# Attention with a gated MLP on one core: seven products one batch earlier, a weight load in halves, zeros multiplied in early waits, a new table of moments

## The chip, the core and the metric

The kernel runs on one core of a Trainium2 chip. The metric is the device time of one execution in microseconds, the median of several runs. The engines are TensorE (PE in the rows; PEld is its weight load), VectorE (DVE), ScalarE (ACT), GpSimd (POOL) and SyncE (SP), which issues most transfers.

## The reference

The reference is causal windowed attention, a gated layer and a spatially gated MLP, one behind the other, for 8 batches of 576 positions and 8 heads of 64:

```python
scores = scale * np.matmul(q, k.transpose(0, 1, 3, 2))   # heads 0-3: window of 32; 4-7: 32 keys, every 4th
attn = softmax(np.where(masks, scores, -1e9));  x = attn @ v          # (B, S, 512)
gate = sigmoid(causal_conv5(x, conv_w));  y = (gate * (x @ w_val)) @ w_out_1
h = relu(y @ w_in);  u, v = h[..., :512], h[..., 512:]
v_n = (v - mean(v)) / sqrt(var(v) + 1e-6)
v_s = einsum('ts,bsd->btd', w_spatial, v_n) + b_spatial[None, :, None]
out = (u * v_s) @ w_out_2
```

The weight matrices (w_val, w_out_1, w_in, w_out_2, conv_w) come as 64-bit floats, 1 MB for each half of a matrix of 512x512; q, k, v and w_spatial are 32-bit.

## The kernel before

A batch goes through two parts. Its attention (`a_...`) takes the 8 heads as 4 pairs: `a_scores` (72 small products into one PSUM buffer `s`), `a_max` (VectorE: scale, mask, row maximum), `a_exp` (ScalarE), `a_sum` (VectorE, then a multiplication on POOL), `a_trans` (in batch 0 products with the identity on TensorE and eight ScalarE copies; later VectorE and small transfers), `a_pv`, `a_split` (a value as a high part that TensorE takes in one pass and a low rest), `a_conv` (five VectorE steps, each on the result of the one before) and `a_tanh`. Then the MLP: `val` (8 tiles of 128x288; in batch 0 four float32 products each, later twelve of high and low parts), `v` and `norm` (5 row blocks), `u`, `sp`, and last `out`.

The last product, with w_out, is done in one of two ways. Up to batch `SEVEN - 1`, `out` does 8 tiles with 12 products each, and ScalarE copies each tile out and stores it. From batch `SEVEN` on the 2x2 block matrix is multiplied with seven block products instead of eight: `sp` subtracts two blocks more, `t` makes three combinations of blocks on VectorE with their high and low parts, `w` does 14 groups of six products, whose results VectorE adds up. `wsum` makes the sums of w_out's blocks that this needs, once.

Weights are loaded in two units each (`load_w`), converted from 64 bits by one ScalarE step (Abs) and four VectorE steps (`from64`, used by `w_f32`, each step on the result of the one before), and for batch 0 two of them are multiplied with each other (`fuse`: w_out_1 with w_in, so that the layer between them falls away; `wm` is w_out_1, in the trace `w_mid`, `wiv` and `wiu` the two halves of w_in, `wv` is w_val).

The order of everything is written out by hand. Each step is a generator; a part runs up to its next `yield`. `EARLY` gives a moment for each part of each step of the first batches, `EVERY` for all later ones (shifted by 74.5 a batch). The loop at the end takes the part with the lowest moment, emits its instructions, and puts the next part back with the higher of its own moment and the one just used. Every engine, and the sync queue with its transfers, then works in exactly the order of emission. Moments have no other meaning: they only sort.

The PSUM pool `ps_m` (tag `m`) has four buffers, which `val`, `v`, `u`, `sp`, `out`, `w`, `fuse` and batch 0's `a_trans` share; `s` and `o` have one buffer each. `qk` and `vv` have two buffers each; unit 0 of `wiu` is loaded into the place of unit 0 of `wv`. In the profile all instructions have line 641, that of the wrapper that records them, so the rows are told apart by their tiles.

Of the kernel before, what the change touches and what calls it, by code (L numbers as in the profile page):

```python
# [28 lines left out]
SEVEN = 2  # L29
# [34 lines left out]
def _swapped(b, x):  # L64
# [11 lines left out]
ORDER = [  # L76
    ("load_qk", 0, 0),
# [111 lines left out]
    ("w_f32", "wiv", 0,): (3.801, 6.907, 7.863, 8.102, 8.341,),
    ("a_sum", 0, 0,): (4.279, 5.951,),  # L190
    ("load_w", "wm", 1,): (4.518,),
    ("a_scores", 0, 1,): (4.757,),
    ("conv_w_f32",): (4.996, 6.668, 7.146, 7.624, 10.013,),
    ("a_max", 0, 1,): (5.235, 5.474,),
    ("a_exp", 0, 1,): (5.712,),
    ("a_pv", 0, 0,): (6.190, 12.403, 15.987,),
    ("load_qk", 0, 2,): (6.429,),
    ("a_trans", 0, 0,): (7.385, 8.819, 9.774, 10.252, 10.730,),
    ("w_f32", "wm", 1,): (8.580, 11.447, 12.642, 15.748, 16.226,),
    ("a_scores", 0, 2,): (9.058,),  # L200
    ("load_mask", 1,): (9.297,),
    ("a_pv", 0, 3,): (9.536, 36.775, 37.253,),
    ("fuse", "wiv", 0,): (10.491, 11.686, 19.571, 20.288, 23.872, 25.783,),
    ("load_w", "wiv", 1,): (10.969,),
    ("a_conv", 0, 0,): (11.208, 17.421, 20.049, 21.721, 22.199, 23.394,),
    ("a_sum", 0, 1,): (11.925, 12.881,),
    ("load_vv", 0, 0,): (12.164,),
    ("a_trans", 0, 1,): (13.120, 13.359, 16.465, 19.810, 20.766,),
    ("a_pv", 0, 1,): (13.598, 25.067, 27.695,),
    ("a_max", 0, 2,): (13.836, 14.075,),  # L210
    ("load_qk", 0, 3,): (14.314,),
    ("a_scores", 0, 3,): (14.553,),
# [12 lines left out]
    ("a_trans", 0, 2,): (22.677, 24.111, 25.306, 25.545, 26.978,),
    ("w_f32", "wv", 0,): (22.916, 23.155, 24.350, 26.739, 28.173,),
    ("a_scores", 1, 0,): (23.633,),
    ("a_exp", 0, 3,): (24.589,),
    ("load_vv", 1, 0,): (24.828,),
    ("fuse", "wiv", 1,): (26.022, 26.261, 27.217, 27.456, 28.412, 30.084,),  # L230
    ("a_sum", 0, 3,): (28.651, 30.562,),
    ("load_bias",): (28.890,),
    ("fuse", "wiv", 2,): (29.129, 31.757, 32.235, 33.907, 38.686, 45.616,),
    ("val", 0, 0, 0,): (29.607, 32.713, 33.191, 37.731, 41.793, 43.943, 45.855,),
    ("a_trans", 0, 3,): (31.040, 31.518, 34.624, 35.341, 35.580,),
    ("a_conv", 0, 1,): (31.279, 33.669, 38.925, 40.598, 47.766,),
    ("a_tanh", 0, 0,): (32.952,),
    ("a_conv", 0, 2,): (33.430, 35.819, 37.969, 40.120, 41.554,),
    ("load_mask", 2,): (34.146,),
    ("load_qk", 1, 2,): (34.385,),  # L240
    ("val", 0, 2, 0,): (34.863, 38.447, 42.270, 42.987, 46.571, 47.527, 56.129,),
    ("load_mask", 3,): (35.102,),
    ("load_w", "wiu", 0,): (36.058,),
    ("a_max", 1, 0,): (36.297, 39.642,),
    ("load_vv", 0, 3,): (36.536,),
    ("a_pv", 1, 1,): (37.014, 87.669, 95.076,),
    ("a_scores", 1, 1,): (37.492,),
    ("val", 0, 1, 0,): (38.208, 39.881, 41.315, 43.465, 49.200, 53.740, 56.607,),
    ("load_w", "wiu", 1,): (39.164,),
    ("a_pv", 1, 0,): (39.403, 73.333, 75.722,),  # L250
    ("w_f32", "wiu", 0,): (40.359, 42.509, 46.332, 48.483, 49.439,),
    ("a_conv", 0, 3,): (40.837, 44.421, 47.288, 50.155, 51.589,),
    ("load_qk", 2, 1,): (41.076,),
    ("val", 0, 3, 0,): (42.031, 44.899, 46.810, 49.678, 55.651, 57.085, 59.952,),
    ("load_sp", 4,): (42.748,),
    ("a_tanh", 0, 2,): (43.226,),
    ("val", 0, 1, 1,): (43.704, 47.049, 49.917, 51.111, 52.545, 57.802, 73.094, 84.563,),
    ("a_exp", 1, 0,): (44.182,),
    ("load_sp", 2,): (44.660,),
    ("split_pair", "wm", 0,): (45.138, 53.979, 61.147, 62.580,),  # L260
    ("val", 0, 3, 1,): (45.377, 48.005, 48.961, 50.872, 54.217, 60.191, 75.483, 89.581,),
    ("load_vv", 1, 2,): (46.093,),
    ("a_tanh", 0, 1,): (48.244,),
    ("split_sp", 4,): (48.722, 68.315, 69.988, 83.129, 83.846, 99.138,),
    ("a_sum", 1, 0,): (50.394, 53.023,),
    ("val", 0, 0, 1,): (50.633, 51.350, 51.828, 52.306, 55.173, 56.846, 68.554, 70.943,),
    ("split_pair", "wiu", 0,): (52.067, 53.262, 54.695, 60.669,),
    ("val", 0, 2, 1,): (52.784, 54.934, 57.324, 57.563, 59.713, 71.421, 72.138, 78.112,),
    ("a_tanh", 0, 3,): (53.501,),
    ("w_f32", "wiu", 1,): (54.456, 58.279, 59.474, 60.908, 61.864,),  # L270
    ("a_trans", 1, 0,): (55.412, 55.890, 56.368, 59.235, 64.253,),
    ("load_sp", 1,): (58.040,),
    ("split_pair", "wm", 1,): (58.518, 63.058, 63.297, 63.536,),
    ("fuse", "wiu", 1,): (58.757, 65.209, 67.359, 68.793, 69.749, 74.288,),
    ("fuse", "wiu", 2,): (58.996, 64.492, 69.271, 75.244, 78.350, 80.501,),
    ("v", 0, 1,): (60.430, 61.386, 64.970, 70.226,),
    ("a_max", 1, 1,): (61.625, 62.819,),
    ("split_pair", "wiu", 1,): (62.102, 62.341, 65.448, 67.598,),
    ("v", 0, 0,): (63.775, 64.731, 70.465, 71.660,),
    ("fuse", "wiu", 3,): (64.014, 66.164, 67.120, 74.050, 77.873, 80.262,),  # L280
    ("fuse", "wiu", 0,): (65.687, 66.642, 67.837, 69.032, 71.899, 78.589,),
    ("a_exp", 1, 1,): (65.926,),
    ("load_sp", 0,): (66.403,),
    ("a_sum", 1, 1,): (66.881, 69.510,),
    ("split_pair", "wv", 1,): (68.076, 76.439, 76.917, 91.970,),
    ("load_vv", 1, 1,): (70.704,),
    ("a_conv", 1, 0,): (71.182, 75.005, 79.545, 81.935, 84.324, 87.191,),
    ("split_sp", 2,): (72.377, 83.607,),
    ("a_scores", 1, 2,): (72.616,),
    ("a_trans", 1, 1,): (72.855, 73.572, 75.961, 76.678, 80.023,),  # L290
    ("split_sp", 0,): (73.811, 85.997,),
    ("load_qk", 1, 3,): (74.527,),
    ("norm", 0, 0,): (74.766, 76.200, 85.041,),
    ("norm", 0, 1,): (77.156, 77.395, 77.634,),
# [392 lines left out]
def attention_gated_mlp_kernel(  # L687
# [902 lines left out]
```

## Time and profile before

| | us |
|---|---|
| median of 3 runs | 649.7 |
| lowest, highest | 648.9, 651.69 |
| the profiled execution | 648.66 |
| its span, first to last instruction | 646.9 |

The profile is that of one execution. The time of that execution is its span and 1.8 us around it. Rows of TensorE need care: a product's duration includes its way through the array, so products that follow each other overlap, and the price of one is the duration of a block divided by its number.

### The profile page before, as it was taken

What the parts mean: (1) busy time and instruction counts of PE and PEld (TensorE: products, weight loads), DVE (VectorE), ACT (ScalarE), POOL (GpSimd) and SP (SyncE); (2) the same over time, 40 slices, a digit from 0 to 9 for tenths busy, and PEclk for the clock granted to TensorE, in tenths of its full rate; (3) what the DMA queues carried; (4) which work ended last, traced back from release to release, by engine and by line L of the source; (5) the groups of instructions that cost most, each with busy time, mean ns of one, the idle gap of its engine ahead of it and who ended that gap; (6) DMA issues with size and microseconds to landing.
All of it is one profiled execution on the core that took longest, in us unless ns stands there. A gap on an engine that the chain in (4) does not pass through costs nothing.

```text
span 646.9 us, 18122 instructions
## 1 busy us (share of the span) xinstructions
PE 626.2 (97%) x7176; PEld 578.5 (89%) x7176; DVE 489.7 (76%) x883; ACT 351.0 (54%) x994; POOL 349.6 (54%) x418
## 2 busy tenths in 40 slices
PE   2899999999999999999999999999999999999997
PEld 2557889998899989999899989999899989999997
DVE  4999878987788787786687967787687967774425
ACT  4967678624444435545476656555476656443422
POOL 1112898746635574575546456375547456455524
PEclk9999999999999999999999999999999999999999
DMA  8953235344331611144213431144214421110002
GB/s 323 412 197 118 56 108 198 113 130 99 80 81 36 184 19 20 41 143 125 76 42 125 118 105 47 19 150 118 75 41 126 119 72 42 19 49 28 2 1 74
DMA packets 85609, 63.61 MB, mean 98 GB/s; under 512 B 64531, under 2 KB 74643, under 8 KB 85013
## 3 DMA queue, kind: packets, MB, share of 16 engines
q1 hardware_dynamic: 76884, 53.60, 28.1%
q10 hardware_dynamic: 8640, 8.85, 3.9%
q8 instruction: 57, 0.93, 0.6%
q14 instruction: 28, 0.22, 0.1%
HBM read 44.92 MB, written 9.44 MB: 84 GB/s over the span
## 4 chain that ended last, share of the span: by engine, by line
PE 92%; DMA 2%; DVE 2%; POOL 1%; ACT 1%; issue 0%; ACTq 0%; SPq 0%; DVEq 0%
PE sp_ps L641 19%; PE u_ps L641 16%; PE v_ps L641 16%; PE val_ps L641 14%; PE w_ps L641 14%; PE o_ps L641 5%; PE s_ps L641 4%; PE out_ps L641 4%; DMA raw<-in_w_mid_t 1%; DMA out<-ob 1%; DVE wiv_f L641 1%; DVE wm_f L641 1%; POOL gl L641 1%; DVE w_sum L641 0%; PE t_ps L641 0%
## 5 line engine op out<-in xcount | busy, mean ns | idle before, releaser
L641 DVE SCALAR_TENSOR_TENSOR tt<-xt,cw,tt 128x576 f32<-128x576 f32 x116 | 104.9, 910 | 13.6 <-ACT tt L641 10.9
L641 PE MATMUL sp_ps<-wsp_h,vh 128*128 128x288 f32 x320 | 93.5, 297 | 0.0
L641 POOL TENSOR_TENSOR g2l<-ru,g2h 128x288 fp32r<-128x288 f32 x64 | 60.5, 961 | 56.5 <-ACT g2h L641 47.6
L641 PE MATMUL u_ps<-gl,w_h 128*128 128x288 f32 x256 | 75.6, 295 | 1.2 <-POOL gl L641 1.2
L641 POOL TENSOR_TENSOR gl<-tt,gh 128x288 fp32r<-128x288 f32 x64 | 56.3, 890 | 37.3 <-ACT gh L641 37.1
L641 PE MATMUL u_ps<-gh,w_h 128*128 128x288 f32 x256 | 76.0, 297 | 0.0
L641 PE MATMUL sp_ps<-wsp_l,vh 128*128 128x288 f32 x256 | 75.4, 295 | 0.0
L641 PE MATMUL sp_ps<-wsp_h,vl 128*128 128x288 f32 x256 | 75.4, 295 | 0.0
L641 PE MATMUL u_ps<-gh,w_l 128*128 128x288 f32 x256 | 75.4, 294 | 0.0
L641 ACT ACTIVATE e_t<-e_t,mx 128x64 f32<-128x64 f32 x207 | 68.9, 336 | 3.4 <-DVE mx L641 2.1
L641 POOL TENSOR_TENSOR e_t<-e_t,sm 128x576 f32<-128x576 f32 x31 | 39.2, 1266 | 56.4 <-DVE sm L641 36.0
L641 PE MATMUL val_ps<-xh,wval_h 128*128 128x288 f32 x224 | 66.7, 298 | 0.2 <-DVE tt L641 0.2
L641 PE MATMUL val_ps<-xh,wval_l 128*128 128x288 f32 x224 | 66.0, 295 | 0.0
L641 PE MATMUL val_ps<-xl,wval_h 128*128 128x288 f32 x224 | 66.0, 294 | 0.0
L641 PEld LDWEIGHTS sp_ps<-wsp_h,vh 128*128 128x128 f32 x320 | 60.0, 188 | 0.8
L641 PE MATMUL v_ps<-w_h,gh 128*128 128x512 f32 x160 | 58.8, 392 | 0.0
L641 PE MATMUL v_ps<-w_l,gh 128*128 128x512 f32 x160 | 58.5, 390 | 0.0
L641 POOL TENSOR_TENSOR rs<-rs,mhalf 128x1 f32<-128x1 f32 x40 | 26.6, 666 | 52.1 <-DVE rs L641 49.4
L641 POOL TENSOR_TENSOR xl<-xt,xh 128x576 fp32r<-128x576 f32 x28 | 42.4, 1516 | 20.8 <-ACT xh L641 20.8
L641 ACT CAST g2h<-ru 128x288 fp32r<-128x288 f32 x64 | 27.0, 432 | 48.5 <-DVE ru L641 34.9
L641 POOL TENSOR_TENSOR vl<-v_t,vh 128x512 fp32r<-128x512 f32 x32 | 43.3, 1362 | 12.9 <-ACT vh L641 12.3
L641 PEld LDWEIGHTS u_ps<-gl,w_h 128*128 128x128 f32 x256 | 48.0, 188 | 2.2 <-POOL gl L641 1.7
(163 smaller groups left out, 1839.0 us busy)
## 6 DMA issues: line engine op xcount, KB each, us to landing
qk_t<-in_qk SPq DMA_DIRECT2D x30, 592.0 KB, 4.3
vv_t<-in_vv SPq DMA_DIRECT2D x30, 384.0 KB, 4.7
out<-ob ACTq DMA_DIRECT2D x38, 144.0 KB, 2.0
raw<-in_w_in SPq DMA_DIRECT2D x4, 1024.0 KB, 8.3
pt<-et SPq DMA_DIRECT2D x240, 16.0 KB, 1.9
out<-ru ACTq DMA_DIRECT2D x22, 144.0 KB, 2.9
pt<-et SPq DMA_DIRECT2D x144, 20.0 KB, 1.8
raw<-in_w_mid_t SPq DMA_DIRECT2D x2, 1024.0 KB, 10.4
```

Of the source, the lines that this page charges most:

```text
L641: ins = self._tc.keep_in_program_order(fn(*args, **kwargs))
```

## The change

Five things are changed.

- `SEVEN` is 1 instead of 2: batch 1, too, does its last product with `t` and `w` in place of `out`, and `wsum` comes in batch 1.
- The load of unit 0 of `wm` is issued as two transfers of 512 KB, and its conversion is done in two halves, ten parts in place of five.
- A tile `zero` of 128x288 is set to zero by VectorE first of all; `warm` multiplies it with itself, 16 times in all, in nine steps, each into a buffer of `ps_m` that nobody reads.
- Every moment in `EARLY` is replaced; `EVERY` is as before. Many parts now have a moment below that of the part ahead of them (often below zero), which makes them follow at once.
- Some entries of `EARLY` go (`out` of batch 1), others come (`wsum`, `warm`).

```diff
-SEVEN = 2
+SEVEN = 1
 ORDER = [
+    ("warm", 0, 2),
...
+    ("warm", 7, 1),
+    ("warm", 8, 1),
     ("load_qk", 0, 0),
...
 EARLY = {
-    ("load_w", "wm", 0,): (0.217,),
-    ("load_ident",): (1.412,),
-    ("w_f32", "wm", 0,): (1.889, 2.367, 3.084, 3.562, 4.040,),
-    ("a_exp", 0, 1,): (5.712,),
-    ("w_f32", "wm", 1,): (8.580, 11.447, 12.642, 15.748, 16.226,),
-    ("a_conv", 0, 2,): (33.430, 35.819, 37.969, 40.120, 41.554,),
-    ("w_f32", "wiu", 0,): (40.359, 42.509, 46.332, 48.483, 49.439,),
...
+    ("warm", 0, 2,): (-133.081,),
+    ("load_w", "wm", 0,): (-73.526, -75.209,),
+    ("warm", 5, 2,): (-56.644,),
+    ("warm", 7, 1,): (-53.220,),
+    ("a_scores", 0, 0,): (-52.205,),
+    ("load_w", "wm", 1,): (-25.599,),
+    ("load_qk", 0, 2,): (-25.305,),
+    ("load_qk", 0, 3,): (-22.397,),
+    ("load_ident",): (-21.606,),
+    ("w_f32", "wm", 0,): (-21.389, -63.873, -71.475, -69.879, -56.098, -100.527, -22.399, -78.854, -44.988, -26.893,),
+    ("a_exp", 0, 0,): (-20.865,),
+    ("w_f32", "wm", 1,): (-2.766, -53.646, -82.714, -12.021, 12.392,),
+    ("a_exp", 0, 1,): (8.085,),
+    ("a_conv", 0, 2,): (39.452, -20.612, -11.415, -61.458, -14.711,),
+    ("w_f32", "wiu", 0,): (40.027, 41.020, 39.149, 47.579, 51.578,),
+    ("a_tanh", 0, 0,): (40.227,),
+    ("a_pv", 0, 3,): (-22.569, 45.022, -30.396,),
+    ("wsum", 1,): (141.159, 148.262, 116.586, 142.348, -3.076,),
+    ("wsum", 3,): (195.850, 138.468, 7.495, 144.068, 125.820,),
...
+            if (key, u) == ("wm", 0):
+                raw[key, u] = t
+                syn.dma_start(out=t[:, 0], in_=src[:, 0])
+                yield
+                syn.dma_start(out=t[:, 1], in_=src[:, 1])
+                return
...
+    def warm(i, n):
+        ps = ps_m.tile([128, 512], F32, tag="m", name="warm_ps")
+        for k in range(n):
+            matmul(ps[:, 0:HS], zero[:, 0:128], zero, True, True)
...
+        if (key, u) == ("wm", 0):
+            a, b = (from64(wide[key][:, m, 0:DM], raw[key, u][:, m]) for m in range(2))
+            for _ in a:
+                yield
+            yield
+            yield from b
+            return
...
+    zero = act.tile([128, S], F32, tag="ru0", name="zero")[:, 0:HS]
+    vec.memset(zero, 0.0)
```

## Rows read from the trace of the kernel before

**Rows 1.** The page, part 1: busy time, share of the span, instructions.

```profile
PE 626.2 (97%) x7176; PEld 578.5 (89%) x7176; DVE 489.7 (76%) x883; ACT 351.0 (54%) x994; POOL 349.6 (54%) x418
```

**Rows 2.** Busy time by stretch: stretch, its length, each engine, granted clock, DMA share.

```profile
0.00:8.00 8.00, 2.16 (x72) 1.92 (x72) 1.32 (x3) 1.28 (x1) 1.89 (x7) 1.00 0.71 229
8.00:16.00 8.00, 2.16 (x72) 1.95 (x72) 5.41 (x9) 5.36 (x21) 0.91 (x1) 1.00 1.02 417
16.00:31.00 15.00, 11.79 (x273) 8.17 (x274) 14.52 (x25) 14.40 (x57) 1.80 (x6) 1.00 1.02 418
31.00:72.00 41.00, 40.62 (x432) 28.59 (x432) 40.47 (x60) 27.88 (x83) 13.34 (x12) 1.00 0.43 143
...
128.00:250.00 122.00, 120.57 (x1367) 112.63 (x1366) 97.27 (x164) 49.72 (x102) 71.08 (x81) 1.00 0.33 88
250.00:600.00 350.00, 350.00 (x3978) 332.40 (x3977) 262.11 (x500) 196.04 (x585) 193.53 (x245) 1.00 0.28 78
600.00:647.00 47.00, 43.01 (x311) 41.92 (x309) 20.33 (x46) 14.87 (x33) 18.77 (x21) 1.00 0.08 26
```

**Rows 3.** TensorE in order of time: start, duration, instructions, idle before and its end.

```profile
4.50 2.16 PE L641 MATMUL s_ps<-qk_t 64*32 64x64 f32 x72 [4.50 <-DMA qk_t<-in_qk]
11.19 2.16 PE L641 MATMUL s_ps<-qk_t 64*32 64x64 f32 x72 [4.54 <-DMA qk_t<-in_qk]
...
19.20 2.16 PE L641 MATMUL s_ps<-qkv 64*32 64x64 f32 x72 [1.19 <-DVE wiv_f L641]
...
30.71 3.70 PE L641 MATMUL w_ps<-wiv_f,wm_f 128*128 128x512 f32 x8 [1.73 <-DVE wiv_f L641]
...
49.73 1.03 PE L641 MATMUL s_ps<-qk_t 64*32 64x64 f32 x72
```

**Rows 4.** The chain that ended last: start, duration, work.

```profile
51.13 13.85 PE val_ps L641 x56
...
66.38 5.45 PE v_ps L641 x24
...
202.93 8.19 PE out_ps L641 x60
...
211.58 3.21 DMA out<-ob
...
226.56 1.31 POOL w_sums L641
```

**Rows 5.** Waits of TensorE from 225 to 250 us: total, times, longest.

```profile
PE u_ps L641 <- POOL gl L641: 1.2, 2, 0.6
```

**Rows 6.** Transfers issued at 1.65, 3.6, 4.76 and 40 to 50 us: size, us to landing.

```profile
raw<-in_w_mid_t SPq DMA_DIRECT2D x1, 1024.0 KB, 7.8
raw<-in_w_in SPq DMA_DIRECT2D x1, 1024.0 KB, 10.1
raw<-in_w_mid_t SPq DMA_DIRECT2D x1, 1024.0 KB, 12.9
raw<-in_w_in SPq DMA_DIRECT2D x2, 1024.0 KB, 6.4
```

**Rows 7.** VectorE in order of time, as rows 3.

```profile
10.67 1.42 DVE L641 TENSOR_SCALAR wm_f<-wm_f 128x1024 f32<-128x1024 f32 x2 [2.42 <-ACT wm_f L641]
...
31.58 0.74 DVE L641 SCALAR_TENSOR_TENSOR e_t<-s_ps,mask_sb 128x576 f32<-128x576 f32 x1
32.24 0.81 DVE L641 SCALAR_TENSOR_TENSOR tt<-o_ps,cw,tt 128x576 f32<-128x576 f32 x1
32.97 0.74 DVE L641 TENSOR_REDUCE mx<-e_t 128x9 f32<-128x576 f32 x1
...
64.58 0.41 DVE L641 SCALAR_TENSOR_TENSOR tt<-tt,val_ps 128x288 f32<-128x288 f32 x1
...
88.55 1.66 DVE L641 SCALAR_TENSOR_TENSOR tt<-o_ps,cw,tt 128x576 f32<-128x576 f32 x2
```

**Rows 8.** VectorE by form: count, busy us, mean ns, idle before.

```profile
L641 DVE TENSOR_TENSOR ru<-ru 128x288 f32<-128x288 f32 x48 | 33.4, 716 | 2.1
...
L641 DVE TENSOR_TENSOR ru<-w_ps,ru 128x288 f32<-128x288 f32 x48 | 20.2, 451 | 4.9 <-PE w_ps L641 4.7
```

More of the change, by code (lines that the diff above doesn't have):

```diff
@@ L76 @@
 ORDER = [
+    ("warm", 0, 2),
+    ("warm", 1, 2),
+    ("warm", 2, 2),
+    ("warm", 3, 2),
+    ("warm", 4, 2),
+    ("warm", 5, 2),
+    ("warm", 6, 2),
+    ("warm", 7, 1),
+    ("warm", 8, 1),
     ("load_qk", 0, 0),
@@ L253 @@
[L253 to L270, printed above, removed]
@@ new lines @@
+    ("warm", 6, 2,): (8.995,),
+    ("load_w", "wv", 1,): (9.227,),
+    ("a_scores", 0, 3,): (9.920,),
+    ("a_sum", 0, 1,): (10.347, 13.354,),
+    ("a_max", 0, 2,): (11.066, -59.406,),
+    ("load_vv", 0, 1,): (12.331,),
+    ("w_f32", "wiv", 1,): (14.326, 3.954, -34.884, -44.589, -35.744,),
+    ("a_exp", 0, 2,): (14.337,),
+    ("a_pv", 0, 0,): (15.469, 5.567, -28.107,),
+    ("load_sp", 0,): (16.631,),
+    ("warm", 4, 2,): (17.412,),
+    ("a_sum", 0, 2,): (17.436, -46.083,),
+    ("load_qk", 1, 0,): (18.886,),
@@ new lines @@
+    ("fuse", "wiv", 1,): (29.101, 35.839, -11.970, -103.245, -62.727, -16.098,),
+    ("fuse", "wiv", 3,): (29.808, -26.519, 35.425, -19.764, -53.811, -45.761,),
+    ("load_vv", 0, 3,): (30.938,),
+    ("warm", 8, 1,): (31.235,),
+    ("load_w", "wiu", 0,): (31.277,),
+    ("a_trans", 0, 2,): (31.900, -107.608, -14.237, -17.687, -7.412,),
+    ("load_qk", 2, 0,): (32.905,),
+    ("load_mask", 2,): (33.692,),
+    ("a_pv", 1, 0,): (36.129, 73.298, -39.382,),
+    ("a_scores", 1, 0,): (37.699,),
@@ new lines @@
+    ("a_exp", 1, 0,): (51.102,),
+    ("a_sum", 1, 0,): (53.227, 5.437,),
+    ("val", 0, 3, 1,): (54.066, 61.463, 27.924, -72.217, -17.183, -114.819, 65.728, 5.826,),
+    ("val", 0, 1, 1,): (54.410, 58.507, 9.188, 25.180, -27.228, 64.645, 9.054, -104.737,),
+    ("val", 0, 0, 1,): (54.924, 55.792, 21.716, 27.762, -26.212, -11.445, -18.340, -0.934,),
+    ("load_w", "wiu", 1,): (55.652,),
+    ("a_tanh", 0, 1,): (57.241,),
+    ("split_pair", "wiu", 0,): (57.995, -8.850, -156.658, -10.448,),
+    ("load_vv", 1, 0,): (59.497,),
@@ new lines @@
+    ("a_tanh", 0, 3,): (60.412,),
+    ("a_scores", 1, 1,): (60.630,),
+    ("a_trans", 1, 0,): (60.939, -24.411, -74.118, -15.202, -6.561,),
+    ("load_sp", 2,): (61.283,),
+    ("val", 0, 1, 0,): (61.592, 45.798, 41.191, 56.575, -29.116, 47.475, -35.541,),
+    ("val", 0, 3, 0,): (61.694, -42.009, 57.378, 26.571, -8.302, 41.674, -35.296,),
+    ("a_max", 1, 1,): (62.672, 4.260,),
+    ("load_qk", 1, 3,): (62.768,),
+    ("w_f32", "wiu", 1,): (63.064, 45.367, -52.766, -1.964, -55.870,),
+    ("a_exp", 1, 1,): (63.250,),
@@ new lines @@
+    ("a_max", 1, 2,): (77.424, 46.091,),
+    ("fuse", "wiu", 1,): (77.544, 41.697, -25.251, 48.685, 75.759, 62.618,),
+    ("split_pair", "wv", 0,): (80.168, 2.943, 22.864, 28.208,),
+    ("load_sp", 3,): (80.820,),
+    ("fuse", "wiu", 3,): (81.633, 51.035, 57.441, -26.236, 61.993, -19.722,),
+    ("a_exp", 1, 2,): (82.331,),
+    ("a_sum", 1, 2,): (83.684, -60.948,),
+    ("v", 0, 3,): (84.147, 38.280, 23.076, -34.161,),
+    ("v", 0, 2,): (84.240, 52.750, 27.078, 38.421,),
+    ("split_sp", 2,): (85.015, -76.083,),
@@ new lines @@
+    ("out", 0, 0, 1,): (133.939, 72.709, 119.259, -9.635, 129.311, 136.218,),
+    ("val", 1, 0, 1,): (134.436, 57.957, 35.430, -9.600, 116.452, 7.404,),
+    ("a_pv", 2, 1,): (137.307, 166.018, 132.259, 103.053, 124.283,),
+    ("a_exp", 2, 1,): (137.656,),
+    ("a_conv", 1, 3,): (137.862, 121.081, 72.426, 33.825, 116.729,),
+    ("load_vv", 2, 0,): (138.425,),
+    ("out", 0, 1, 1,): (140.305, 145.332, 72.091, -109.201, 7.638, 28.106,),
+    ("a_sum", 2, 1,): (140.705, 101.931, 130.304,),
+    ("wsum", 1,): (141.159, 148.262, 116.586, 142.348, -3.076,),
@@ new lines @@
+    ("out", 0, 3, 1,): (142.405, 81.041, 22.743, 51.806, 68.185, 114.723,),
+    ("out", 0, 2, 1,): (143.732, 96.815, 20.917, 71.792, 62.815, 42.813,),
+    ("load_vv", 2, 1,): (144.781,),
+    ("a_tanh", 1, 3,): (144.893,),
+    ("val", 1, 0, 0,): (146.335, 132.559, 74.204, 59.640, 122.474,),
+    ("a_tanh", 1, 2,): (148.217,),
+    ("a_trans", 2, 1,): (148.888, 154.163, 95.085, 97.005, 124.904,),
+    ("val", 1, 3, 0,): (148.963, 75.747, 122.810, 100.075, 11.898,),
+    ("wsum", 2,): (149.263, 57.592, 30.470, 1.168,),
@@ new lines @@
+    ("load_vv", 3, 1,): (204.639,),
+    ("a_split", 2, 2,): (205.390, 46.399,),
+    ("a_split", 2, 3,): (206.734, 185.085,),
+    ("a_scores", 3, 1,): (209.834,),
+    ("a_max", 3, 1,): (212.570, 198.306, 165.959,),
+    ("a_exp", 3, 1,): (212.870,),
+    ("val", 2, 1, 0,): (213.658, 196.234, 60.472, 231.006, 145.035,),
+    ("val", 2, 0, 0,): (213.780, 110.568, 194.418, 228.138, 147.650,),
+    ("a_conv", 2, 3,): (215.870, 224.539, 83.113, 135.151, 211.280,),
+    ("a_sum", 3, 1,): (216.330, 137.050, -10.343,),
@@ L527 @@
+    ("a_conv", 3, 3,): (295.528, 215.556, 280.711, 231.583, 296.195,),
+    ("a_tanh", 3, 1,): (297.415,),
+    ("a_tanh", 3, 3,): (299.281,),
 }
```

555 lines of the change are left out of this document (243 added, 312 removed), and 18 rows, old and new, of the table EARLY.

## The prediction

> **What bounds the kernel now.** I read the page's busy shares first: TensorE is busy 626.2 of 646.9 us [rows 1]. A gain therefore has to take work from TensorE or fill its waits, and the next view, busy time by stretch, shows where those are [rows 2]: 11.7 us in the first 16 us, 3.2 from there to 31, 0.4 to 72, 1.4 between 128 and 250, none from 250 to 600, and some 4 at the end, which the change leaves alone. Then the instructions of TensorE in order of time [rows 3]. It is made to wait in the first 31 us, and its clock is low there: 72 score products take 2.16 us at 4.5, 11.2 and 19.2 us, and 1.03 us at 49.7 us, so that they ran at the lower level (1.2 GHz) and later at 2.4 GHz; the clock rose during the unbroken work that begins at 19.2 us. (The granted clock in [rows 2] reads 1.00 in each stretch, the first too; here the durations decide.) From 30.71 us on TensorE runs almost without a break. VectorE is full too: 14.5 of 15 us up to 31, 40.5 of 41 up to 72 [rows 2], and DMA is full from 8 to 31 us. So up to 72 us two engines and the loads are all near their limits, and what ends last is decided by order; behind 72 us it is TensorE alone.
>
> **The change, part by part.**
>
> *Seven products in batch 1.* Eight tiles of twelve products (96) become fourteen groups of six (84). Sixty `out` products take 8.19 us [rows 4], 0.137 us each, so twelve fewer are worth 1.6 us of TensorE. VectorE gets 8 more SBUF additions or subtractions of 128x288 (two in `sp`, six in `t`) and 14 that read `w_ps`: 8 x 0.716 + 14 x 0.451 = 12.0 us [rows 8]. On ScalarE eight copies of `out` go and eight come (six of t, two of p1); POOL gets six more subtractions. VectorE has 24.7 us free between 128 and 250 us [rows 2], so most of the 12 us is covered; if the cover is gone at the wrong place, each PSUM buffer that a `w` holds longer stops TensorE. No row shows this density, since before batch 2 carried it. I take 0.4 us, between 0 and 2.5.
>
> *The sums of w_out's blocks.* They are now due at 141 to 196 instead of behind batch 1's `out`. In the chain of waits that place is a real stall: ScalarE's copies of `out` wait for their own stores (3.21 us), so the sums come late, and POOL's part of the last one (1.31 us at 226.56) stands just ahead of the low parts `gl`, for which the first `u` of batch 2 waits 1.2 us [rows 4, 5]. The stores of `out` are gone from batch 1 and the sums are early: I take the 1.2 us as gained, at least 0 (if another wait stands there), at most 1.4.
>
> *Zeros on TensorE.* Sixteen products of 128x288. The nearest row is 56 float32 products of that size in 13.85 us, 0.25 us each at 2.4 GHz [rows 4], so about 0.5 at 1.2. Five stand ahead of the first scores: 2.5 us, and TensorE is idle until 4.50 us; the rest lie in later waits. If that cover were gone they would cost 4 to 8 us. They can raise the clock from the second score block or earlier, 1.1 us for each of three blocks, but what follows these is a wait for a load or for VectorE, so the gain reaches the end only as an earlier start of VectorE.
>
> *The first weight unit in halves.* It lands at 1.65 + 7.8 = 9.5 us [rows 6], and VectorE's first step on it starts at 10.67 [rows 7]. The first half should land near 7.5 us (half its bytes; an estimate), and VectorE's two microseconds on it then fill its wait. ScalarE still does both halves' Abs ahead of the first softmax, so the first row sums wait about 1 us. Counting VectorE's waits up to 31 us: 9.7 us before (6.7 + 2.6 + 0.5, rows 2), about 7.3 after: 2.4 us gained.
>
> *The new order, first 72 us.* I sorted both tables by the moment at which each part is really issued (a part is never issued before the one ahead of it, so the many negative moments mean "at once") and walked the queues. Three things speak against a gain. First, loads: by the sizes of the loads ahead of it and its own, the second half of w_mid is complete at 4.67 MB (4.59 before), so it still lands near 4.76 + 12.9 = 17.7 us [rows 6]; its Abs now stands ahead of the softmax of pair 1 on ScalarE, which so starts only behind that load, near 19 us. The identity, formerly landed long before its use, is behind 5.9 MB. Second, VectorE: before, two chains alternate; now the four steps of a weight unit, or of a convolution, follow each other. An operation that does not need the one ahead of it starts 0.66 to 0.73 us after it though it takes 0.74 to 0.81, while two convolution steps that depend on each other take 1.66 us, 0.83 each [rows 7]. That is 0.10 us for each dependent neighbour, and up to the first `v` I count about 30 more of them: 3.0 us lost. Third, the first `v` needs the gated halves of all four chunks; VectorE ends the last one before at 64.58 + 0.41 = 65.0 us [rows 7], hence now at 65.0 - 2.4 + 3.0 = 65.6 (66.3 added up operation by operation). With ScalarE's high part and POOL's low part behind it, the two first `v` end near 71.7 us. Before they end at 66.38 + 5.45 = 71.8 us [rows 4], with 0.7 us of weight products done that now come later. So TensorE leaves this stretch 0.5 us behind; what the warm clock and the halves bring goes into waits, of which I expect some 10 us between 36 and 62 us (ahead of the values of pair 2, of the fourth `val` product, and of a PSUM buffer for `val`). Bounds: 3.5 us ahead (no price for neighbours, w_mid landing earlier) to 6 behind.
>
> The Trainium skill (VectorE: DVE Perf Modes, Terms, "DRAIN") says that the next operation can't issue until the pipe has emptied. By that the order of the chains would cost nothing. The trace disagrees: neighbours overlap by 0.08 us, unless one needs the other [rows 7]. By the rule the start would be 2.5 us ahead; that is the first rival.
>
> **Sum.** The profiled execution took 648.66 us (its span is 646.9): 648.66 - 1.6 - 1.2 + 0.5 + 0.4 = 646.8 us. It stands 1.0 us under the median of 649.7, so on that scale 647.8 us.
>
> **Rivals.** (1) The start is gained: chains back to back are no dearer and loads come as wished, so that VectorE's 2.4 us and 1 us of TensorE's own reach the end. For it speaks that TensorE's waits up to 31 us are 14.9 us and its cold score blocks cost 3.4 us more; against it, rows 7. Then the start is 3.2 us better than above: 644.6. (2) Slower: ScalarE's Abs of the first half of wiu is queued ahead of the tanh and of pair 3's copy, and its load can only start when `wv` is converted (near 40.6 us). Alone it takes 6.4 us [rows 6]; in the crowded stretch such a load took 10.1 to 12.9. From a landing later than 51 us on, ScalarE, the fourth `val` product and VectorE all stand behind it, and each further microsecond is lost, to which comes the same for wiu's second half, whose issue waits on the sync queue behind a load of qk that needs pair 1's scores done. Six microseconds: 653.8. (3) VectorE becomes the bound of batch 1's end, with its 12 us more: +2.5, 650.3. (4) TensorE waits 4 us near 36 us; in the first 20 us waits of 4.5 us stand between blocks that all ran at 1.2 GHz [rows 3]. If the clock falls there, about 5 us of products up to pair 3's values take twice as long, and 2.5 us of that reach VectorE: +2.5, 650.3. The Trainium skill (TensorE: Matmul & The Clock Gate, Part 1) says that the clock does fall back after an idle stretch; no row shows it falling after it had risen.
>
> **How the numbers follow.** Forecast 0.42, rival 1 0.30, rival 2 0.12, rivals 3 and 4 0.08 each. Faster by over 0.5%, about what a measurement of this kernel can tell from no change, is under 646.5 us: rival 1 and the lower edge of the forecast, 0.35. Slower (over 652.9): rival 2 and tails, 0.14. The rest, 0.51, is the same. The forecast's own range is 646 to 650; to hold eight in ten it must take in rivals 1, 3 and 4: 643.2 to 651.5.
>
> **What would show it.** Right: score blocks near 1.1 us from the second on; TensorE waits between 36 and 62 us; the first `v` near 66 us with a wait inside it; no wait for `gl` behind 220 us; 12 fewer products. Wrong: TensorE unbroken from 28 us or sooner (rival 1), VectorE waiting between 45 and 60 us (rival 2), a new wait for VectorE's `w` additions near 200 us (rival 3), score blocks back at 2.1 us after 36 us (rival 4).

## The result: 657.8 us against 650.0, about 1% slower

The changed kernel takes 657.82 us (median, 656.1 to 657.99) against 650.02 us before (648.9 to 651.69): a ratio of 1.010, with a 95% interval of 1.008 to 1.012 (the two medians alone would give 1.012). The prediction said 647.8 us and kept 643.2 to 651.5, so it missed both the sign and the range. The profiled execution took 656.38 us with a span of 654.6 us, 7.7 us more than before. Where times of different comparisons are set against each other below, I go by their ratios to the kernel before, measured beside them, at 6.5 us per 0.01.

The page of the changed kernel, part 1 (busy time, share, instructions), and the first line of part 4 (shares of the chain that ended last), with the same line of the kernel before under it:

```profile
PE 636.1 (97%) x7196; PEld 582.8 (89%) x7196; DVE 503.7 (77%) x910; ACT 351.5 (54%) x995; POOL 351.3 (54%) x424
...
PE 72%; DVE 11%; POOL 4%; DMA 3%; SPq 3%; issue 3%; ACT 2%; DVEq 0%; POOLq 0%; ACTq 0%
...
PE 92%; DMA 2%; DVE 2%; POOL 1%; ACT 1%; issue 0%; ACTq 0%; SPq 0%; DVEq 0%
```

TensorE is still busy 97% of the span, as in [rows 1]: the share hides the change. The chain hints at it: it runs through something else than TensorE for 28% of the span, 8% before. (TensorE can work beside such a piece of the chain, so this is not lost time.) Next the busy time by stretch, columns as in [rows 2]:

```profile
0.00:8.00 8.00, 6.33 (x82) 4.28 (x82) 1.42 (x7) 1.85 (x3) 1.99 (x10) 1.00 0.76 234
8.00:16.00 8.00, 5.57 (x79) 4.47 (x80) 7.66 (x15) 5.12 (x21) 1.19 (x2) 0.61 1.02 412
16.00:31.00 15.00, 12.02 (x283) 8.32 (x282) 14.29 (x20) 12.93 (x55) 1.19 (x2) 0.98 1.02 418
31.00:72.00 41.00, 41.00 (x428) 27.84 (x427) 38.95 (x57) 30.21 (x96) 13.02 (x12) 1.00 0.42 146
...
128.00:250.00 122.00, 116.57 (x1254) 108.62 (x1250) 103.19 (x176) 49.26 (x101) 72.08 (x85) 1.00 0.33 87
```

Three things differ from [rows 2]. Up to 31 us TensorE idles 7.1 us in place of 14.9, yet gains nothing by it, as the next view shows. The granted clock reads 0.61 between 8 and 16 us; it read 1.00 there before, but since the score blocks then took 2.16 us, the time at the lower level (1.2 GHz), the low clock is seen here and isn't new. And between 128 and 250 us TensorE loses 5.4 of 122 us, where it lost 1.4, while VectorE has 103.2 us of work instead of 97.3. TensorE's start, in order of time (as rows 3), and behind it the first `v` of the kernel before:

```profile
1.22 5.17 PE L647 MATMUL warm_ps<-zero 128*128 128x288 f32 x10 [1.22 <-DVE mhalf L647]
6.32 1.23 PE L647 MATMUL s_ps<-qk_t 64*32 64x64 f32 x72
10.43 2.16 PE L647 MATMUL s_ps<-qk_t 64*32 64x64 f32 x72 [2.88 <-DMA qk_t<-in_qk]
12.52 5.17 PE L647 MATMUL warm_ps<-zero 128*128 128x288 f32 x12
18.74 1.23 PE L647 MATMUL s_ps<-qkv 64*32 64x64 f32 x72 [1.05 <-DMA qkv<-in_qk]
...
28.83 6.28 PE L647 MATMUL w_ps<-wiv_f,wm_f 128*128 128x512 f32 x14
...
67.77 0.40 PE L647 MATMUL v_ps<-w_h,gh 128*128 128x512 f32 x1
...
66.21 0.39 PE L641 MATMUL v_ps<-w_h,gh 128*128 128x512 f32 x1
```

Five zero products are ten rows: a float32 product of this size stands in the trace as two. They end at 6.4 us, so the first scores begin 1.8 us later than in [rows 3]; these run at the higher clock (1.23 us), the second scores, after a wait of 2.88 us, at the lower one again (2.16 us). All sixteen zero products keep TensorE busy for 13.6 us, up to 37 us. Against that stand 8.2 us less idle time up to 72 us and some 3 us (an estimate: what is left over) from score blocks and other products that now run at the higher clock. So the first `v` comes later: it begins at 67.77 us, before at 66.21 with three more weight products done (0.23 us each), which makes 1.56 + 0.68 = 2.2 us behind. One execution is a rough measure here: with the order of the kernel before up to 72 us and no zeros the first `v` begins at 65.2 to 67.5 us in seven traces, 66.2 on average; with the new order and no zeros (seven traces of the runs below) at 66.6, with all zeros (three) at 67.8. So by these averages the new order itself is 1.1 us behind, with its three products fewer, and the zeros add as much again.

The list of TensorE's waits (total, times, longest) is where most of the rest went:

```profile
PE s_ps L647 <- DMA qk_t<-in_qk: 2.9, 1, 2.9
PE out_ps L647 <- ACT ob L647: 2.5, 1, 2.5
PE sp_ps L647 <- DVE ru L647: 2.1, 2, 1.9
PE u_ps L647 <- DVE v_t L647: 1.3, 1, 1.3
...
PE sp_ps L647 <- DVE vh L647: 0.8, 1, 0.8
...
PE val_ps L647 <- POOL xt L647: 0.4, 1, 0.4
```

Behind 72 us four of them are new: 1.3 us at 103 us (`u`), 2.5 at 141 (`out`), 0.8 at 191 and 2.1 at 120 and 204 (`sp`), 6.7 us together. The waits for `gl` of [rows 5] are gone, as forecast. So 2.2 + 6.7 - 1.2 (the waits for `gl`) - 1.6 (the twelve products, as priced in the prediction) = 6.1 of the 7.7 us; 0.4 of the rest is the wait for `xt`, at 300 us, and the cause of the remaining 1.2 stays open.

What TensorE waited for at 141 us, on ScalarE in order of time:

```profile
135.50 0.40 ACT L647 COPY ob<-out_ps 128x288 f32<-128x288 f32 x1
137.15 0.38 ACTq L647 DMA_DIRECT2D out<-ob  x1
137.56 0.40 ACT L647 COPY ob<-out_ps 128x288 f32<-128x288 f32 x1 [1.66 <-DMA pt<-et]
139.23 0.34 ACTq L647 DMA_DIRECT2D out<-ob  x1
139.67 0.40 ACT L647 COPY ob<-out_ps 128x288 f32<-128x288 f32 x1 [1.70 <-DMA pt<-et]
143.13 0.40 ACT L647 COPY ob<-out_ps 128x288 f32<-128x288 f32 x1 [3.07 <-DMA out<-ob]
```

Each store is issued 1.3 us after its copy has ended, when one of the attention block's transfers lands, and the fourth copy waits 3.07 us for a store, because there are two `ob` tiles. And at 204 us, on VectorE:

```profile
194.25 3.38 DVE L647 SCALAR_TENSOR_TENSOR tt<-xt,cw,tt 128x576 f32<-128x576 f32 x4
197.55 0.82 DVE L647 TENSOR_TENSOR ru<-sp_ps,ru 128x288 f32<-128x288 f32 x2
198.28 0.68 DVE L647 TENSOR_TENSOR w_sum<-wout_h 128x512 f32<-128x512 f32 x1
199.00 3.15 DVE L647 TENSOR_TENSOR w_sum<-w_sum,wout_l 128x512 f32<-128x512 f32 x2
...
203.70 1.71 DVE L647 TENSOR_TENSOR e_t<-e_t,mx 128x576 f32<-128x576 f32 x1
205.34 0.45 DVE L647 TENSOR_TENSOR ru<-sp_ps,ru 128x288 f32<-128x288 f32 x1
```

Between two products with `sp` VectorE does a sum of weights and a softmax, from 198.28 to 205.34; the four PSUM tiles fill up and TensorE stops for 1.9 us.

### The profile page after: what moved, and what is told of

Read it like the earlier page. It is cut to its first block, busy times and chain, and to the rows that moved or that the text cites. A ratio compares the mean times of both kernels' runs of the same rounds, so it can differ in the third digit from the quotient of the medians.

```text
span 654.6 us, 18215 instructions
## 1 busy us (share of the span) xinstructions
PE 636.1 (97%) x7196; PEld 582.8 (89%) x7196; DVE 503.7 (77%) x910; ACT 351.5 (54%) x995; POOL 351.3 (54%) x424
## 4 chain that ended last, share of the span: by engine, by line
PE 72%; DVE 11%; POOL 4%; DMA 3%; SPq 3%; issue 3%; ACT 2%; DVEq 0%; POOLq 0%; ACTq 0%
PE val_ps L647 14%; PE sp_ps L647 13%; PE w_ps L647 12%; PE u_ps L647 12%; PE v_ps L647 12%; PE o_ps L647 4%; PE s_ps L647 3%; SPq L647 3%; DVE tt L647 3%; DMA raw<-in_w_out 2%; DMA out<-ob 1%; DVE w_sum L647 1%; PE warm_ps L647 1%; DVE wm_f L647 1%; DVE e_t L647 1%
## 5 line engine op out<-in xcount | busy, mean ns | idle before, releaser
L647 PE MATMUL val_ps<-xh,wval_h 128*128 128x288 f32 x224 | 66.6, 297 | 0.0
L647 PE MATMUL val_ps<-xl,wval_h 128*128 128x288 f32 x224 | 66.2, 296 | 0.4 <-POOL xt L647 0.4
L647 PEld LDWEIGHTS u_ps<-gh,w_h 128*128 128x128 f32 x256 | 48.0, 188 | 2.5 <-issue 1.5
L647 PE MATMUL v_ps<-w_h,gl 128*128 128x512 f32 x128 | 50.0, 391 | 0.2 <-POOL gl L647 0.2
```

The lines of the kernel that those rows point to most:

```text
L647: ins = self._tc.keep_in_program_order(fn(*args, **kwargs))
```

## Experiments

Theory A: the loss has two parts that have nothing to do with the seven products, zeros at the start and places in the new order where the work of VectorE, ScalarE or a queue stands in the way. Rival B: batch 1 now has more work for VectorE than fits, whatever the order.

### Parts of the order

The order is a table of moments, so one can take the parts that one kernel issues before a time T in its order, and all others behind them in the order of the other kernel.

**g72**: the order of the changed kernel up to 72 us, with its zeros and halves, then that of the kernel before (against the changed kernel; the moments are left out).

```diff
-SEVEN = 1
+SEVEN = 2
...
```

> The start alone: the first 72 us of the new order, with the zeros and the first weight unit in two halves; everything later, and the products of batch 1, as in the kernel before. Theory A (the start lost about 2.3 us by 72 us, read from how far TensorE's work was behind the kernel before at that time, and nothing later gives it back): 652 to 653 us. Rival B (the kernel before has slack after 72 us that takes the late start up): 650 us, no difference. Rival C (the start gained, as one rival of the prediction had it): 645 to 647 us.

665.3 us, ratio 1.024 (1.021 to 1.027). TensorE's waits between 72 and 120 us:

```profile
PE o_ps L659 <- DMA pt<-et: 10.5, 2, 9.9
```

**h80**: the complement, the order of the kernel before up to 80 us, then that of the changed kernel (against the kernel before; the moments are left out).

```diff
-SEVEN = 2
+SEVEN = 1
...
```

> The complement: the first 80 us as in the kernel before (no zeros, one whole first weight unit), from 80 us on the new order with seven products in batch 1. Theory A (the rest lost about 5 us by itself: the stall at 103, the one at 140 for the output tile, the ones at 191 to 204 for VectorE): 655 us, so that this and the start alone add up to the whole change's 7.8 us. Rival B (the late losses only follow from the late start, since a buffer comes free later): 650 us or below.

657.9 us, 1.013 (1.009 to 1.016), with a wait of 4.6 us for the same transfers at 94 us. Both runs have a wait where the two orders meet that neither kernel has, so neither total decides anything. They do teach that a few transfers late in the sync queue cost 5 to 10 us of waits, and the low clock behind them more (0.72 in g72 from 96 to 120 us).

**b_seven**: seven products in the order of the kernel before, with only the four sums at their new moments (one of them shown).

```diff
-SEVEN = 2
+SEVEN = 1
...
-    ("wsum", 1,): (192.464, 211.149, 171.551, 159.767, 192.127,),
+    ("wsum", 1,): (141.159, 148.262, 148.262, 148.262, 148.262,),
...
```

> Seven products in batch 1 alone, in the order of the kernel before; only the four sums of weights stand at the new, earlier moments, since batch 1 needs them, and the products of batch 1 replace its eight. Theory A (12 products of 0.137 us each leave TensorE and the waits at 230 us go; the VectorE work added is covered): 646.5 to 648.5 us. Rival B (VectorE gets 12.0 us more work between 128 and 250 us and TensorE waits for it, whatever the order): 651 to 654 us.

667.0 us, 1.026 (1.023 to 1.030). TensorE's waits from 190 to 240 us, and busy time in a stretch of them, the granted clock third from the end:

```profile
PE w_ps L633 <- DVE ru L633: 3.4, 1, 3.4
PE w_ps L633 <- ACT g2h L633: 3.0, 1, 3.0
PE w_ps L633 <- DVE ob L633: 2.3, 1, 2.3
...
220.00:232.00 12.00, 8.30 (x38) 8.13 (x39) 11.47 (x21) 2.88 (x6) 5.10 (x5) 0.66 0.43 123
```

The `w` products follow `sp` with nothing between them that TensorE could do while the operands are made. This is rival 3 of the prediction, at 8.7 us of waits instead of 2.5, and the whole run is 17 us slower: behind the waits the granted clock falls as well (0.78 from 200 to 212 us, 0.90 to 220, 0.66 to 232), which makes another 7.5 us of full speed missing (an estimate: 12 x 0.22 + 8 x 0.10 + 12 x 0.34). In this form, with only the sums moved, the change would have been far worse than with its new order. It doesn't tell order from load, though.

### The zeros and the halves

**a_nowarm**: the changed kernel without zeros.

```diff
-    ("warm", 0, 2),
...
-    ("warm", 8, 1),
```

> The changed kernel without any of the zero products. Theory A (the five ahead of the first scores hold these back by 1.8 us, and the clock falls back after them anyway): 656 us, 1 to 2 us faster than with them. Rival B (the zeros keep the clock up and pay for themselves): 659 us or more. Rival C (the start waits for a transfer either way): the same 657.8 us.

654.4 us, 1.006 (1.004 to 1.009): 2.5 us faster than with the zeros, by the ratios. Theory A, and more than its 1 to 2 us. By the averages above about half of it is there at the first `v`; where the other half goes isn't shown. The waits behind 60 us stay:

```profile
PE out_ps L629 <- ACT ob L629: 2.7, 1, 2.7
PE sp_ps L629 <- DVE ru L629: 2.1, 2, 1.9
PE u_ps L629 <- DVE v_t L629: 1.4, 1, 1.4
```

**b_warm5**: the kernel before with the first five zeros.

```diff
+    for k in range(5):
...
+        matmul(ps[:, 0:HS], zero[:, 0:128], zero, True, True)
```

> The kernel before with only the five zero products ahead of the first scores. Theory A (they take 5.2 us at the lower clock and end after the first scores' operands have landed, so the first scores end about 1 us later, and what follows moves by that): 650.5 to 651.5 us. Rival B (the second scores wait for their own transfer to 11 us anyway, so nothing moves): 649.8 us. Rival C (the first scores run at the higher clock, and that pays): 648.5 us or less.

649.7 us, 0.9995 (0.998 to 1.001): nothing. Its TensorE in order of time:

```profile
6.31 1.62 PE L641 MATMUL s_ps<-qk_t 64*32 64x64 f32 x72
11.08 2.16 PE L641 MATMUL s_ps<-qk_t 64*32 64x64 f32 x72 [3.14 <-DMA qk_t<-in_qk]
```

and busy time by stretch, the granted clock third from the end:

```profile
8.00:16.00 8.00, 2.16 (x72) 1.95 (x72) 6.74 (x10) 5.36 (x21) 0.97 (x1) 0.66 1.02 408
16.00:24.00 8.00, 6.88 (x124) 4.48 (x124) 7.80 (x16) 7.59 (x31) 1.74 (x6) 0.50 1.03 422
```

The zeros raise the clock, a wait of 3.14 us follows, and the products up to 24 us run at the lower level as they did without zeros.

**a_zfirst** and **a_zlate**: the changed kernel with the five first zeros only, and with the eleven later ones only (lines of the table taken out as above).

> The changed kernel with only the five zero products that stand ahead of the first scores. Theory A (those five end while the operands of the first scores and then of the second are being loaded, as they did in the kernel before, where they changed nothing): 654 to 655 us, as without any zeros. Rival B (they are the ones that cost, by holding back the first scores): 657 us or more.

655.3 us, 1.0075 (1.005 to 1.010).

> The changed kernel with only the eleven zero products behind the second scores. Theory A (the six at 12.5 us take 5.2 us at the lower clock and push the third scores and what follows behind their operands): 657 us, as with all zeros. Rival B (they lie in TensorE's waits): 654 to 655 us.

659.6 us, 1.0125 (1.010 to 1.015; one of its four executions took 655.6). The eleven later ones cost 4.0 us against a_nowarm, the five first ones 0.7, which the intervals don't separate from nothing. Theory A in both. That eleven cost no less than all sixteen fits the clock: in a_zlate it falls at 26 us, where 24 products with values take 2.04 us in place of 1.21 and two zero products 2.04 in place of 1.24, 1.6 us together; with all sixteen it falls at 10 us, ahead of zeros. The intervals of the two runs overlap, so this is a reading of the traces and not shown by the times.

**a_nohalf**: a_nowarm with the first weight unit whole.

```diff
-            if (key, u) == ("wm", 0):
-                raw[key, u] = t
-                syn.dma_start(out=t[:, 0], in_=src[:, 0])
-                yield
-                syn.dma_start(out=t[:, 1], in_=src[:, 1])
-                return
...
```

> The changed kernel without the zeros and with the first weight unit in one transfer and five steps again, in the same order otherwise. Theory A (the halves bring the first conversion forward by nothing that TensorE waits for, since its waits of the first 35 us end on the scores' operands and on the second weights): 654 us, the same as without the zeros alone. Rival B (the halves are worth their 0.5 to 1 us): 655 us. Rival C (their five more steps on VectorE are the 1.2 us that the start is still behind): 653 us.

653.7 us, 1.005 (1.003 to 1.007): no difference from a_nowarm. The halves do fill VectorE (7.69 of 8 us between 8 and 16 us in a_nowarm, 6.35 in a_nohalf), but nothing that sets the end was waiting for that.

### The late waits

**a_fix3**: a_nowarm with three moments moved.

```diff
-    ("a_conv", 1, 1,): (67.737, 95.476, 90.235, -31.519, 50.162, 85.244,),
+    ("a_conv", 1, 1,): (67.737, 95.476, 95.5, 97.1, 97.11, 97.12,),
...
-    ("a_trans", 2, 0,): (121.330, 80.972, 34.367, 44.426, 140.979, 55.160,),
+    ("a_trans", 2, 0,): (121.33, 121.34, 131.395, 134.502, 145.971, 146.21,),
...
-    ("wsum", 3,): (195.850, 138.468, 7.495, 144.068, 125.820,),
+    ("wsum", 3,): (145.0, 145.01, 145.02, 147.5, 148.0,),
```

> The changed kernel without the zeros, with three moments put elsewhere, one for each late stall of TensorE: the transfers of the attention block (2, 0) issued after the stores of the first output tiles instead of before them (stall of 2.7 us at 140 us), the sum of weights 3 at 145 instead of 198 us (stall of 2.0 us at 202 us), and the filter chain (1, 1) cut in two around the two additions for v (stall of 1.4 us at 103 us). Theory A (each stall has the cause named, and TensorE sets the end, so that the gains add up): the three waits are gone from the list of waits and the time falls by 6 us from the 654.4 us without zeros, to 648 to 649 us. Rival B (VectorE is the bound of these stretches and the waits move on to the next product): 652 to 654 us. Rival C for the stall at 140 us (the two buffers of the output tile are too few, whoever issues first): that wait stays, and the time falls by 3.5 us, to 651 us.

652.6 us, 1.004 (1.003 to 1.006). The waits at 103 and 202 us are gone and the one at 140 us is 1.3 us, but a wait of 0.9 us stands at 117 us. Of 6 us expected 1.3 came by the ratios. The profiled execution is 3.3 us faster, but it is the fastest of ten, with a granted clock of 1.000 where six of the ten have 0.996 or 0.997 (another one at 1.000 took 653.2). The time is rival B's; of the waits, two are gone.

**a_ob3**: a_nowarm with a third `ob` tile.

```diff
-            o = rot.tile([128, HS], F32, tag="ob", name="ob")
+            o = rot.tile([128, HS], F32, tag="ob", bufs=3, name="ob")
```

> The changed kernel without the zeros, with three buffers instead of two for the output tile, and no moment moved. Theory A (the stores at 135 to 142 us wait for the transfers issued ahead of them in the program's order, not for a buffer): the wait of out_ps at 140 us shrinks by less than 1 us, 653.5 to 654.5 us. Rival C (two buffers are too few): the wait of 2.7 us is gone, 651.5 to 652 us.

652.6 us, 1.004 (1.002 to 1.005). The wait for `ob` is not in the list any more, which is rival C, though 1.8 us came by the ratios and not 2.4 to 2.9. The number of tiles decides; moving the transfers halved the wait in a_fix3 and did nothing for it in h100_fix, below. Why a store on one queue waits for transfers on another wasn't tried.

**a_fix4**: both together.

> The changed kernel without the zeros, with the three moved moments of the run before and three buffers for the output tile. Theory A (the wait of 1.4 us left at 140 us is the output tile's buffer and nothing takes its place): 651 to 651.5 us against 652.6 us without the third buffer. Rival B (TensorE is held by VectorE right behind it): 652.6 us as before.

650.7 us, 0.9997 (0.998 to 1.002), as fast as the kernel before. Of the 6.7 us that the change lost, the zeros are 2.5 and these four edits 4.4. TensorE's waits between 60 and 330 us:

```profile
PE val_ps L629 <- DVE tt L629: 1.1, 1, 1.1
PE sp_ps L629 <- DVE ru L629: 0.8, 1, 0.8
PE sp_ps L629 <- DVE vh L629: 0.3, 1, 0.3
PE v_ps L629 <- POOL gl L629: 0.3, 1, 0.3
```

6.2 us of waits have become 2.5, and the largest, at 154 us, is new: VectorE there stands 1.4 us for POOL, which still reads the tile that sum 2 overwrites.

**z_fix4**: a_fix4 with all zeros.

> The changed kernel with all its zeros, with the three moved moments and the third buffer for the output tile. Theory A (zeros and stalls cost apart from each other): 654 us, 3.5 us more than without the zeros. Rival B (the zeros only make the later stalls longer): 651 us.

651.8 us, 1.002 (1.001 to 1.004). Zeros cost 1.6 us here, 2.5 on the order with the waits; the intervals don't tell these two apart, but 3.5 us it isn't.

### Products or load

**a_seven2**: a_nowarm with eight products again in batch 1, its outputs at the moments of the kernel before.

```diff
-SEVEN = 1
+SEVEN = 2
+    ("out", 1, 0, 0,): (204.196, 204.196, 204.196,),
...
```

> The changed kernel without the zeros and with eight products again in batch 1 (its outputs at the moments that they had in the kernel before; the sums of weights stay early). Theory A (the new order holds the loss, the seven products of batch 1 are a gain of 1.6 us): 655 to 656.5 us, above the 654.4 us with seven. Rival B (the extra work on VectorE holds the loss): 651 to 652.5 us, since the wait of 2.0 us at 202 us goes with it.

657.4 us, 1.010 (1.007 to 1.013), against 1.006 (1.004 to 1.009): theory A, and against B, which had 651 to 652.5: with less work for VectorE (93.6 us between 128 and 250 us, 103.8 in a_nowarm) it is 2.4 us slower. The two intervals together allow anything from nothing to 5 us, but the five executions (657.35 to 659.59) all lie above those of a_nowarm (653.96 to 655.08). The profiled execution has a granted clock of 0.83 from 140 to 150 us that a_nowarm's has not; executions with an equal mean clock of 0.999 stand as far apart (657.4 against 654.0 and 654.1, with 0.4 us between the kernels before that were measured beside them). The sums stay early in this run, so it says what the products are worth, not what the sums' new place costs.

**h100_fix**, **h140_fix**, **h140_fix2**, **h140_fix5**: the order of the kernel before up to 100 or 140 us, then the changed one, with sum 3 at 145 us (in the first with the transfers of a_fix3, in the others with three `ob` tiles); in the third one load goes back to its old place, and the fourth has sums 2 and 4 later as well.

```diff
-    ("load_qk", 2, 3,): (140.0016,),
+    ("load_qk", 2, 3,): (152.422,),
```

```diff
-    ("wsum", 2,): (149.263, 149.263, 149.263, 149.263,),
+    ("wsum", 2,): (152.0, 152.01, 152.02, 152.03,),
...
```

> The first 100 us in the order of the kernel before (no zeros, one whole first weight unit), from there the new order with seven products in batch 1, with the moments for the stalls at 140 and 202 us moved as above. Theory A (start and the three stalls are all that the new order lost, and the 12 products saved are worth 1.6 us): 646.5 to 648.5 us, faster than the kernel before. Rival B (the extra work on VectorE costs more than the products saved, whatever the order): 650 us or more.

653.4 us, 1.006 (1.003 to 1.008): a wait of 2.7 us for `ob` at 140 us is there although the transfers stand later.

> Seven products in batch 1 on a sound base: everything up to 140 us in the order of the kernel before (no zeros, one whole first weight unit), from there the new order, with the sum of weights 3 at 145 us and three buffers for the output tile. Theory A (12 products of 0.137 us and the wait of 1.6 us at 246 us go, and the extra work on VectorE fits): 646.5 to 648 us. Rival B (VectorE's 12 us more between 128 and 250 us cost more than that, in whatever place): 650 us or more.

650.5 us, 1.000 (0.998 to 1.002).

> Seven products in batch 1 on the order of the kernel before up to 140 us, as in the run before of this kind, with one load put back to where the kernel before has it: the operands of the scores (2, 3), which on SyncE's queue stood ahead of the attention block's transfers and waited 2.4 us for a score buffer, so that TensorE waited 2.7 us at 146 us. Theory A (nothing else is lost, and the products saved are worth 1.6 us or a little more): 647.5 to 648.5 us, faster than the kernel before. Rival B (the extra work on VectorE takes it back elsewhere): 650 us.

652.1 us, 1.003 (1.001 to 1.004): the wait at 146 us (2.0 us in the trace of h140_fix) is gone, and waits of 0.5 and 1.9 us stand at 151 and 154, one of 1.1 at 294.

> The order of the kernel before up to 140 us and seven products in batch 1 behind it, with the sums of weights 2 and 4 three microseconds later. Theory A (the waits of 0.6 and 2.1 us at 151 to 155 us were VectorE standing at the first step of sum 2 for GpSimd): 649 to 649.5 us. Rival B (VectorE's load): 651 to 652 us.

649.5 us, 1.001 (0.999 to 1.002). Those are gone in turn but for 0.4 us at 151, and between 140 and 170 us stand:

```profile
PE u_ps L633 <- ACT gh L633: 2.0, 1, 2.0
PE u_ps L633 <- POOL gl L633: 0.5, 1, 0.5
```

**a_fix5**: a_fix4 with sums 2 and 4 later in the same way, and two steps of a conversion, with what follows them, behind the first `sp`.

```diff
-    ("w_f32", "wo", 1,): (108.916, 59.441, 12.735, 50.917, -16.122,),
+    ("w_f32", "wo", 1,): (108.916, 108.92, 108.93, 114.3, 114.31,),
...
```

> The changed kernel without the zeros, with the three moved moments and the third buffer of the run before of this kind, and two more places mended: the sums of weights 2 and 4, whose first operation on VectorE waited 1.4 and 1.0 us for GpSimd with the products for val behind it (wait of TensorE of 1.3 us at 154 us), stand three microseconds later, and the last two steps of one conversion for w_out stand behind the first products of sp (wait of 0.9 us at 117 us). Theory A (these waits too are places in VectorE's order and not its load): 648.5 to 649.5 us, faster than the kernel before by up to 0.3%. Rival B (VectorE's load is what holds TensorE, and each wait taken away comes back at the next place): 650.5 to 651 us, as without these two.

652.4 us, 1.0045 (1.003 to 1.006): slower than a_fix4. Both waits aimed at are gone; TensorE's waits from 120 to 170 us:

```profile
PE out_ps L629 <- POOL g2l L629: 1.6, 1, 1.6
PE u_ps L629 <- ACT gh L629: 0.8, 1, 0.8
PE u_ps L629 <- POOL gl L629: 0.5, 1, 0.5
```

and busy time by stretch, columns as before:

```profile
128.00:132.00 4.00, 2.41 (x11) 2.13 (x11) 3.97 (x7) 1.02 (x4) 4.00 (x5) 0.80 0.41 152
132.00:136.00 4.00, 4.00 (x90) 3.74 (x89) 3.90 (x6) 3.76 (x7) 4.00 (x4) 0.77 0.08 13
```

So rival B is half right. The products are no loss, and no single wait is forced; but from 100 to 165 us VectorE is free for 6.3 of 65 us in a_fix4 (9.0 before), and the ten VectorE steps of the sums with their ScalarE and POOL parts, moved into it, came back as a wait somewhere each time. POOL and ScalarE are free for 18 and 32 us there, so it is not their load. Not each small wait is the order's doing, either: h140_fix and h140_fix2 have the same order up to 140 us, and only the first shows a wait of 1.2 us, at 100 us. None of these versions is faster than the kernel before; a_fix4, h140_fix and h140_fix5 can't be told from it.

## Why the prediction was wrong, point by point

- **Twelve products, -1.6 us: right in sign.** a_seven2 puts them at 2.4, with intervals that allow 1.6 and reach down to nothing.
- **The wait for `gl`, -1.2 us: right.** It is gone.
- **The start, +0.5 us: mis-sized.** 2.2 us in the trace, inside its bounds. The order alone would be 1.1 by the averages above, the zeros are the other half, and it is they that were mis-sized. They were priced from 56 rows as 56 products; they are two rows each, so a product takes 1.03 us at the lower clock and not 0.5, the five end at 6.4 and not before 4.5 us, and "TensorE is idle until 4.50" covers 3.3 of their 5.2 us. All sixteen came to 13.6 us, not "4 to 8", and that price should have been weighed. The walk of the loads came true: the first half's Abs starts at 7.66 us, that of w_mid's second half at 17.19 and the softmax of pair 1 at 18.24. The 10 us of waits expected between 36 and 62 us did not come, and the `v` came later than 66 us. Of the halves' 2.4 us on VectorE 1.3 are seen, and they reach nothing (a_nohalf).
- **VectorE fuller, +0.4 us (0 to 2.5), and nothing for the new order behind 72 us: the step that failed.** The four waits behind 72 us are 6.7 us, four edits to three moments and one buffer give 4.4 us back. I walked the new order up to 72 us only, and for the rest used the average: VectorE free 24.7 of 122 us, "TensorE alone" behind 72 us. But the new table had moved everything up to 300 us, and a wait comes from what stands ahead of one product, not from a share: VectorE still has 18.8 us free in that stretch. And the largest of the four, at 141 us, is no VectorE wait at all; ScalarE's stores had a row in the list already (3.21 us in [rows 4]) and I took it as gone.
- **Rivals.** Rival 1's sign came (TensorE unbroken from 25.2 to 72 us) without its time: TensorE had spent 13 us on zeros, most of them at the lower clock, and the sign can't tell that from a gain. Its 3.2 us are also not the sum of its parts: from 0.5 behind to 2.5 ahead is 3.0, to 2.4 + 1 ahead 3.9. Rival 2 did not happen; VectorE idles 2.0 us from 31 to 72 us. Rival 3 is half of the truth, 2.7 us at 191 to 204 us, behind `sp` rather than `w`. Rival 4's fall of the clock came at 10 us and not at 36. The Trainium skill (TensorE: Matmul & The Clock Gate, Part 1) says that the clock falls back after an idle stretch; the trace of before had no row for it, that of after does (0.61 between 8 and 16 us, where a wait of 2.88 us stands).
- **The range** took in the forecast and three rivals, all of them for terms that I had seen. There was no term for the new order behind 72 us, and 0.14 for slower was what was left over.

## What to carry over

When a change brings a new order, walk all of it that moved, queue by queue, before pricing any term; an engine's average free time covers nothing at the one place where a buffer waits for it. Filler work on an engine must be priced at the clock at which it will run and must end before the real operands land. And taking waits away one at a time recovers less than their sum: 6 us of them gave 1.3 with three edits and 4.4 with four.

## What the hardware showed that I had not expected

- **Two engines at one memory.** A VectorE operation with both inputs in SBUF takes very different times; one with an input in PSUM doesn't. From the changed kernel (minimum, median, maximum in ns; first and last start; form):

```profile
L647 DVE TENSOR_TENSOR ru<-sp_ps,ru x64: 397/450/459, 119.7 to 639.4; 128x288 f32<-128x288 f32 x64
L647 DVE TENSOR_TENSOR ru<-ru x56: 397/512/1373, 205.9 to 645.8; 128x288 f32<-128x288 f32 x56
```

Sorted by whether POOL computes during at least 30% of the operation: `ru<-ru` takes 794 ns on average with POOL (40 of them) and 452 without (16); `ru<-sp_ps,ru` 443 with and 452 without. The same holds for the sums of weights (1182 against 674 ns). The Trainium skill (SBUF — State Buffer, "SBUF: two separate sides") says that VectorE, with two SBUF inputs, and a GpSimd operation that reads SBUF hold a shared pair of ports in turn, the other one fully blocked. The trace agrees (794 against 452 ns). So the 0.716 us of [rows 8] is a mean over two prices, and sums placed beside POOL's work, as between 199 and 202 us, cost nearly twice as much.
- **Granted clock and time.** The kernel before itself took 647.7 to 649.7 us in the twelve executions of the last comparison with a mean granted clock of 0.998 or more, and 649.8 to 651.8 us in the ten at 0.993 to 0.997; in three of the other four comparisons the two ranges overlap, and in all four the means of the two groups are 1.6 to 2.6 us apart. A wait can cost more than itself in this way: in a_fix5 1.6 us at 128 us are followed by a clock of 0.80 and 0.77. It isn't every wait: behind that for `ob` near 141 us it is 0.83 from 140 to 150 us in a_seven2, a_zfirst and a_zlate and 1.00 in a_nowarm and the changed kernel, so one execution's trace is no sure price of a wait.
